# A new hand-off list for the first three blocks of a fused retention and snake-MLP kernel

## The chip, the cores and the metric

One NeuronCore of a Trainium2 chip runs the whole kernel. The metric is the device time of one execution in microseconds. The engines are named as in the profile: PE (TensorE, matmuls), PEld (its weight loads), DVE (VectorE), ACT (ScalarE), POOL (GpSimd) and SP (SyncE, which here only issues DMAs). Each engine works through its own instructions in order.

## The reference

`q`, `k` and `v` have 8 batches, 8 heads, 576 positions and 64 features, in float32. The first part is retention (attention without softmax, with a decay); its output is the input of the second part, a dense MLP with a snake activation:

```python
scores = scale * np.matmul(q, k.transpose(0, 1, 3, 2))
gamma = 1.0 - 2.0 ** (-5.0 - np.arange(H, dtype=np.float32))
Dmat = np.where(rel >= 0, gamma[:, None, None] ** rel[None, :, :], 0.0)
x = np.matmul(scores * Dmat, v)          # then transposed to 4608 tokens x 512
h = x @ w_in                             # 512 -> 2048
s = np.sin(alpha * h)
g = h + s * s / (alpha + 1e-09)
out = g @ w_out                          # 2048 -> 512
```

## The kernel before

The 4608 tokens are worked off in nine blocks of 512. Blocks 0 to 7 are the first 512 positions of each batch; block 8 gathers the last 64 positions of all batches. All matmuls are in float16 with float32 sums in PSUM.

**Attention of one block** (class `Attention`). A half `p` of a block is 256 positions. `load` brings q, k or v of a half in (SP's queue, 512 KB) and `cast` multiplies it by powers of the decay and by the scale and writes float16 (for v it is a copy alone); the argument `ys` casts one half of the heads. In blocks 0 and 1 `turn` transposes q and k on TensorE and `take` copies the result out of PSUM; from block 2 on `crossed` has the DMA transpose them. `scores` multiplies k and q, `masked` applies the causal mask on VectorE, `outer` makes the sums of k times v per chunk of 128 positions, `take_sum`, `evict` and `evict_bank` bring these to SBUF, `more` (GpSimd) or `next_sum` (VectorE) adds the decayed sum of the chunk before, and `to_state` writes the state in float16. `values` and `add_states` add up the output in PSUM, and `keep` copies it to SBUF as x of the block.

**MLP of one block.** A unit is 128 of the 2048 hidden columns. `project(n, u, bank)` is four matmuls of 512 columns (or two halves of 256), `sine` runs on ScalarE, `square` on an engine that the list names, `product` on VectorE, and it frees the unit's PSUM bank. `gemm2(n, u, bank)` is one quarter of the sum of one output tile of 128 tokens (tile `u // 4`, hidden units `4 * (u % 4)` to `4 * (u % 4) + 3`); `finish` copies the tile out and stores it.

**PSUM** has six tags: `op`, `h0`, `h1`, `h2` are one bank each, `m0` and `m1` two banks each. A tile with a tag waits until what stood there was read.

**The order.** For blocks 0 to 2 everything above is written out as one list of calls, inside `tc.manual_schedule()`: each engine gets its instructions in the list's order, and waits between engines are put in from the data. From block 3 on a loop makes the order; it is the same before and after. Buffers in SBUF are taken in the order in which the list asks for them, by the table `BUFFERS`: the digit is the number of the buffer. `load_w_in(g)` and `load_w_out(g)` bring a quarter of the weights each through GpSimd's queue, with a cast to float16 on the way. `wait_for_w_in(g)` and `wait_for_w_out(g)` are tiny DMAs on SP that read the loaded weights, so that SP's later loads stay behind them. `keep_busy` are matmuls on zeros at the start, when TensorE has nothing to do.

Of the kernel before, what the change touches and what calls it, by code (L numbers as in the profile page):

```python
# [19 lines left out]
    "raw": "012345012345012345102405314023140240124012401240",  # L20
    "k16": "0123012302131313",
    "q16": "0120120121202020",
    "v16": "0123012310230123",
    "kT": "0123012310232323",
    "qT": "0123013210232323",
    "kvs": "00000000",
    "s16": "01010101",
    "xT": "01202020",
    "s32": "010101010101010101010",
    "ret": "01230123012313020213021302130213",  # L30
    "s": "012312013021302130210213021302130231032032103102320132013201320132013201320132013201320132013201320132013201320132013201320132013201320132013201",
    "ss": "012302130123012032103213021302103210321031203120312031203120312031203120312031203120312031203120312031203120312031203120312031203120312031203120",
# [4 lines left out]
def kernel(  # L37
# [23 lines left out]
    P = 128  # L61
# [221 lines left out]
    class Attention:  # L283
# [83 lines left out]
        def more(self, c):  # L367

            s32 = place("s32", [P, 4, D], F32)
            nc.gpsimd.tensor_tensor(s32, self.kvs[:, c - 1], g1.unsqueeze(2).to_broadcast([P, 4, D]), MULT)  # L370
            nc.gpsimd.tensor_tensor(self.kvs[:, c], s32, self.kvs[:, c], ADD)  # L371
# [180 lines left out]
    ops = {}  # L552
    PART = {None: slice(0, 512), 0: slice(0, 256), 1: slice(256, 512)}
# [46 lines left out]
    def gemm2(n, u, tag, cols=slice(0, 512)):  # L600
        c, part = divmod(u, 4)
        if (n, c, cols.start) not in ops:
            ops[n, c, cols.start] = psum.tile([P, 512], F32, tag=tag, bufs=1, name="ops")
        for fk in range(4 * part, 4 * part + 4):
            matmul(  # L605
                ops[n, c, cols.start][:, cols], gT[n][:, fk, c * P : (c + 1) * P], w_out16[:, fk, cols],
                start=(fk == 0), stop=(fk == FC - 1), skip_group_check=True,
            )
# [127 lines left out]
    def wait_for_w_in(g):  # L736

        nc.sync.dma_start(gate, w_in16[g][:, 0, 0:64])
# [42 lines left out]
    with tc.manual_schedule():  # L781
# [27 lines left out]
        at[0].outer((0,), "h1", "h2")  # L809
        keep_busy(8, "op", 256)  # L810
        cast(0, "k", 1, G_, (1,))
        take(0, "k", 0, A_)
        take(0, "q", 0, A_)
        at[0].scores(0, 0, "m0")
        at[0].scores(0, 1, "m1")
# [5 lines left out]
        turn(0, "k", 1, "op")  # L821
        take(0, "k", 1, A_, (0,))
        take(0, "k", 1, A_, (1,))
        turn(0, "q", 1, "h0")
        take(0, "q", 1, A_)
        keep_busy(3, "op")
        at[0].scores(1, 0, "m1")
        keep_busy(1, "h1")
# [8 lines left out]
        take(1, "q", 1, A_)  # L837
        at[0].masked(0, 1)
        at[0].next_sum(1)
        at[0].to_state(1, G_)  # L840
        load_w_out(2)
        at[0].outer((1,), "h2", "h0")
        at[0].take_sum(3, A_)
        at[0].masked(0, 0)
        at[0].values(0, False, "m1")
        at[0].values(0, True)
        at[0].masked(1, 0)
        at[0].masked(1, 1)
        at[0].next_sum(2)
        at[0].to_state(2, V)  # L850
        at[0].add_states(0)
        at[0].keep(0, A_, V)
        at[0].values(1, False, "h1", "h0")
        at[0].values(1, True)
        at[0].add_states(1)
        load(1, "q", 0)
        cast(1, "q", 0, G_)
        load_w_in(3)
        turn(1, "q", 0, "op")
        at[0].keep(1, V, A_)  # L860
        take(1, "q", 0, V)
        project(0, 2, "h2", 0)
        project(0, 3, "m0", 0)
        project(0, 2, "h2", 1)
        sine(0, 2)
        project(0, 3, "m0", 1)
        sine(0, 3)
        square(0, 3, V)
        product(0, 3)
        project(0, 1, "h0", 0)  # L870
        project(0, 1, "h0", 1)
        sine(0, 1)
        square(0, 1, V)
        square(0, 2, A_)
        product(0, 2)
        product(0, 1)
        project(0, 6, "h1")
        sine(0, 6)
        project(0, 7, "m1")
        sine(0, 7)  # L880
        project(0, 0, "op")
        square(0, 7, A_)
        sine(0, 0)
        square(0, 6, V)
        product(0, 7)
        product(0, 6)
# [568 lines left out]
```

## Time and profile before

| what | value |
|---|---|
| median of three runs | 295.57 us (295.13 to 298.53) |
| profiled execution | 295.48 us |
| its span, first to last instruction | 293.8 us |
| granted TensorE clock | 0.998 |
| busy: PE, DVE, ACT, POOL | 282.6, 227.5, 206.4, 135.2 us |
| first projection of block 0 | 21.0 us |
| DMA | 50.08 MB, mean 170 GB/s |

Busy is the sum of an engine's instructions, waits left out. The rows of groups have the form: line, engine, operation, what is written and read with shapes, count, then busy us and mean ns, then idle us before them and what ended most of it. In a timeline a row begins with its start and its length.

### The profile page before, as it was taken

How to read it: one execution, taken by the hardware profiler on the slowest of the kernel's cores; microseconds unless marked ns; L12 is line 12 of the kernel's file. 1: busy time of each engine (PE TensorE's matmuls, PEld its weight loads, DVE VectorE, ACT ScalarE, POOL GpSimd, SP SyncE). 2: the span in 40 equal slices, each digit the busy share in tenths (PEclk: the TensorE clock that was granted, in tenths of full speed). 3: DMA queues.
4: the chain of work that ended last, by engine and by line, in shares of the span. 5: the costliest groups of instructions: out<-in, count | busy, mean ns of one | idle time of the engine just before them, and what ended most of it. 6: DMA issues, size and time to landing. Idle time of an engine off the chain costs nothing. (4 is left out here: it accounts for less than half of the span.)

```text
span 293.8 us, 8462 instructions
## 1 busy us (share of the span) xinstructions
PE 282.6 (96%) x3480; PEld 182.6 (62%) x3480; DVE 227.5 (77%) x336; ACT 206.4 (70%) x340; POOL 135.2 (46%) x152
## 2 busy tenths in 40 slices
PE   6789999999998999999999999999999999999994
PEld 4566555555544654455767777676666676777783
DVE  2597968788349979698987697769777987987784
ACT  2679945997594896787867986797678657865500
POOL 6694776475689576640397039802960000000000
PEclk9999999999999999999999999999999999999999
DMA  7999999999798899968868976897764102111213
GB/s 218 347 235 211 249 292 309 235 261 291 184 219 199 155 173 190 284 120 174 158 160 237 138 190 155 252 126 178 183 176 60 40 9 83 36 38 36 71 38 107
DMA packets 122918, 50.08 MB, mean 170 GB/s; under 512 B 79872, under 2 KB 120832, under 8 KB 122880
## 3 DMA queue, kind: packets, MB, share of 16 engines
q1 hardware_dynamic: 118928, 44.78, 63.8%
q0 software_dynamic: 2688, 4.19, 7.9%
q10 hardware_dynamic: 1264, 0.58, 0.8%
q8 instruction: 27, 0.44, 0.6%
q14 instruction: 11, 0.09, 0.1%
HBM read 36.75 MB, written 9.44 MB: 157 GB/s over the span
## 5 line engine op out<-in xcount | busy, mean ns | idle before, releaser
L592 DVE SCALAR_TENSOR_TENSOR gT<-ss,inva,hps 128x512 f16<-128x512 f16 x144 | 105.4, 743 | 29.7 <-ACT ss L585 26.0
L576 ACT ACTIVATE s<-hps,alpha_t 128x512 f16<-128x512 f32 x144 | 96.6, 681 | 44.7 <-PE hps L568 42.7
L568 PE MATMUL hps<-xT,w_in 128*128 128x512 f16 (+1 forms) x532 | 121.1, 372 | 1.2 <-DMA w_in<-in_moe_w_in_dram 0.6
L568 PEld LDWEIGHTS <-w_in 128*128 128x128 f16 x596 | 66.6, 114 | 51.0 <-issue 1.4
L585 ACT ACTIVATE ss<-s 128x512 f16<-128x512 f16 x106 | 66.6, 631 | 2.8
L605 PE MATMUL ops<-w_out,gT 128*128 128x512 f16 x192 | 46.8, 380 | 0.0
L671 PEld LDWEIGHTS <-gT 128*128 128x128 f16 x384 | 37.5, 98 | 8.3
L207 POOL TENSOR_TENSOR k<-raw,cn 128x1024 f16<-128x1024 f32 (+1 forms) x17 | 28.6, 1682 | 9.7 <-DMA raw<-in_k_dram 9.7
L671 PEld LDWEIGHTS <-S 128*128 128x128 f16 x288 | 27.7, 98 | 5.3
L605 PEld LDWEIGHTS <-gT 128*128 128x128 f16 x192 | 18.0, 98 | 20.5
L363 POOL TENSOR_TENSOR s<-kvs,cn 128x256 f16<-128x256 f32 x17 | 10.8, 639 | 38.7 <-DVE S L652 24.7
L207 POOL TENSOR_TENSOR q<-raw,cn 128x1024 f16<-128x1024 f32 x13 | 24.8, 1912 | 5.8 <-DMA raw<-in_q_dram 4.1
L671 PE MATMUL hps<-T,gT 128*128 128x256 f16 x192 | 22.9, 273 | 0.0
L671 PE MATMUL hps<-w_out,gT 128*128 128x256 f16 x192 | 22.9, 273 | 0.0
L671 PE MATMUL hps<-w_out,S 128*128 128x256 f16 x192 | 22.8, 273 | 0.0
L401 DVE TENSOR_TENSOR ret<-sc,mask 128x1024 f16<-128x1024 f32 x16 | 19.1, 1218 | 2.1 <-PE sc L389 2.0
L120 ACT CAST xT<-o 128x1024 f16<-128x1024 f32 (+1 forms) x15 | 16.5, 1128 | 2.7 <-PE o L451 2.7
L587 DVE TENSOR_TENSOR ss<-s 128x512 f16<-128x512 f16 x29 | 14.7, 509 | 3.2 <-ACT s L576 3.1
L371 POOL TENSOR_TENSOR kvs<-s,kvs 128x256 f32<-128x256 f32 x21 | 15.3, 730 | 2.8 <-DVE kvs L122 1.2
L717 DVE TENSOR_TENSOR osb<-hps,low 128x512 f32<-128x512 f32 x13 | 9.0, 692 | 9.3 <-PE hps L671 9.3
L370 POOL TENSOR_TENSOR s<-kvs,cn 128x256 f32<-128x256 f32 x21 | 13.3, 634 | 6.2 <-ACT kvs L120 6.0
L652 DVE TENSOR_TENSOR S<-gT,S 128x1024 f16<-128x1024 f16 x24 | 15.5, 683 | 0.0
(83 smaller groups left out, 272.2 us busy)
## 6 DMA issues: line engine op xcount, KB each, us to landing
raw<-in_q_dram SPq DMA_DIRECT2D x16, 512.0 KB, 4.9
out_dram<-osb SPq DMA_DIRECT2D x32, 256.0 KB, 2.5
raw<-in_k_dram SPq DMA_DIRECT2D x8, 512.0 KB, 6.4
raw<-in_v_dram SPq DMA_DIRECT2D x8, 512.0 KB, 5.9
raw<-in_v_dram SPq DMA_DIRECT2D x32, 128.0 KB, 3.2
raw<-in_k_dram SPq DMA_DIRECT2D x32, 128.0 KB, 3.1
w_in<-in_moe_w_in_dram POOLq DMA_DIRECT2D x4, 512.0 KB, 11.7
w_out<-in_moe_w_out_dram POOLq DMA_DIRECT2D x4, 512.0 KB, 13.0
```

Source lines behind the costliest of these rows:

```text
L120: eng.copy(d_, s_)
L207: eng.tensor_tensor(dst[:, a0:a1].rearrange("p a r t d -> p t (a r) d"), t_.rearrange("p (t a) x -> p t a x", t=2)[:, :, a0:a1].rearrange( ...
L371: nc.gpsimd.tensor_tensor(self.kvs[:, c], s32, self.kvs[:, c], ADD)
L401: nc.vector.tensor_tensor(ret.rearrange("p t (z x) -> p (t z) x", z=2)[:, :, 0:n], sc.rearrange("p t (z x) -> p (t z) x", z=2)[:, :, 0:n], ...
L568: matmul(hps_of[n, fc][0][:, cols], w_in16[fc // 4][:, a, fc % 4 :: 4], xs[n][:, a, cols], start=(a == 0 and part != 1), stop=(a == KT - 1 ...
L576: nc.scalar.activation(s_t, hps, mybir.ActivationFunctionType.Sin, bias=0.0, scale=alpha_t[:, fc : fc + 1],)
L585: nc.scalar.activation(ss_t, s_t, mybir.ActivationFunctionType.Square)
L587: eng.tensor_tensor(ss_t, s_t, s_t, MULT)
L592: nc.vector.scalar_tensor_tensor(gT[n][:, fc, :], ss_t, inva[:, fc : fc + 1], hps, MULT, ADD)
L605: matmul(ops[n, c, cols.start][:, cols], gT[n][:, fk, c * P : (c + 1) * P], w_out16[:, fk, cols], start=(fk == 0), stop=(fk == FC - 1), sk ...
L652: return eng.tensor_tensor(out_, x, y, op)
L671: matmul(acc[:, 256 * j : 256 * j + 256], lhs[:, x, 128 * j : 128 * j + 128], rhs[:, x], start=(tag is not None and j == js[0] and p == 0 ...
```

## The change

The list of blocks 0 to 2 is replaced by another one, found by a search over a model of the engines and queues. The same calls are in it, with these differences. The loads of block 0 come in another order. GpSimd issues the first three groups of w_in after half a cast of q instead of after k's casts. VectorE casts k of block 0 and, later on, parts of k and q of blocks 2 to 4; casts are more often halved. VectorE has 16 squares instead of 11, ScalarE 23 instead of 28, GpSimd 9 as before. VectorE makes three of the chunk sums (`more` gets an engine) and seven states instead of one. Units, `gemm2` quarters and attention steps follow one another in another order and on other banks; `gemm2` may now add up its four quarters in any order. Buffers get other numbers. `make_mask_halved` moves from the start to block 1. The loop from block 3 on, and the tail, are not touched.

```diff
 BUFFERS = {
-    "raw": "012345012345012345102405314023140240124012401240",
+    "raw": "423104350312251304250124323152014240124012401240",
...
-        def more(self, c):
+        def more(self, c, eng=nc.gpsimd):
             s32 = place("s32", [P, 4, D], F32)
-            nc.gpsimd.tensor_tensor(s32, self.kvs[:, c - 1], g1.unsqueeze(2).to_broadcast([P, 4, D]), MULT)
-            nc.gpsimd.tensor_tensor(self.kvs[:, c], s32, self.kvs[:, c], ADD)
+            eng.tensor_tensor(s32, self.kvs[:, c - 1], g1.unsqueeze(2).to_broadcast([P, 4, D]), MULT)
+            eng.tensor_tensor(self.kvs[:, c], s32, self.kvs[:, c], ADD)
...
+        done = parts_of.setdefault((n, c), [])
+        done.append(part)
         for fk in range(4 * part, 4 * part + 4):
             matmul(
                 ops[n, c, cols.start][:, cols], gT[n][:, fk, c * P : (c + 1) * P], w_out16[:, fk, cols],
-                start=(fk == 0), stop=(fk == FC - 1), skip_group_check=True,
+                start=(len(done) == 1 and fk == 4 * part), stop=(len(done) == 4 and fk == 4 * part + 3),
+                skip_group_check=True,
             )
...
-        keep_busy(7, "op", 128)
-        keep_busy(6, "h0", 256)
-        keep_busy(11, "op", 128)
-        make_mask_halved()
-        load(0, "k", 0)
-        load(0, "q", 0)
-        load(0, "v", 0)
-        cast(0, "k", 0, V, (0,))
-        cast(0, "k", 0, G_, (1,))
-        turn(0, "k", 0, "op")
-        cast(0, "q", 0, V, (1,))
-        cast(0, "q", 0, V, (0,))
-        turn(0, "q", 0, "h0")
-        load(0, "k", 1)
-        cast(0, "k", 1, G_, (0,))
-        invert_alpha()
-        cast(0, "v", 0, A_)
...
-        cast(0, "k", 1, G_, (1,))
...
-        load(0, "q", 1)
-        load_w_in(0)
-        load(0, "v", 1)
-        at[0].take_sum(0, A_)
-        cast(0, "q", 1, V)
...
-        cast(0, "v", 1, A_)
-        load(1, "q", 1)
-        cast(1, "q", 1, G_)
-        at[0].scores(1, 1, "m0")
-        turn(1, "q", 1, "h1")
...
+        load(0, "k", 0)
+        keep_busy(4, "h1", 256)
+        cast(0, "k", 0, V, (0,))
+        cast(0, "k", 0, V, (1,))
+        turn(0, "k", 0, "h0")
+        keep_busy(13, "op", 128)
+        keep_busy(5, "op", 128)
+        load(0, "q", 0)
+        cast(0, "q", 0, V, (1,))
+        load(0, "q", 1)
+        cast(0, "q", 0, G_, (0,))
+        load(0, "k", 1)
+        load_w_in(0)
+        turn(0, "q", 0, "h2")
+        load(0, "v", 0)
+        load(0, "v", 1)
+        take(0, "k", 0, V, (0,))
+        take(0, "k", 0, V, (1,))
+        cast(0, "q", 1, V, (1,))
+        load_w_in(1)
+        load_w_in(2)
+        cast(0, "q", 1, V, (0,))
...
+        cast(0, "k", 1, V, (0,))
+        cast(0, "k", 1, V, (1,))
...
+        cast(0, "v", 0, G_, (0,))
+        cast(0, "v", 0, G_, (1,))
+        cast(0, "v", 1, G_, (0,))
...
+        load(1, "q", 1)
+        cast(0, "v", 1, A_, (1,))
+        at[0].take_sum(1, A_)
+        at[0].take_sum(0, V)
+        at[0].more(1)
...
+        at[0].to_state(0, A_)
+        at[0].take_sum(2, A_)
+        at[0].more(2)
...
+        at[0].to_state(2, V)
+        at[0].values(1, False, "m0")
+        at[0].add_states(0)
+        wait_for_w_in(0)
+        at[0].values(1, True)
+        at[0].add_states(1)
+        load(1, "k", 0)
+        at[0].keep(0, V, A_)
+        at[0].keep(1, V, A_)
+        project(0, 3, "h1", 0)
+        project(0, 3, "h1", 1)
+        load(1, "q", 0)
+        cast(1, "q", 1, V)
+        invert_alpha()
...
+        at[1].take_sum(2, A_)
+        at[1].masked(1, 1)
+        at[1].more(2, V)
+        load(2, "q", 1)
+        make_mask_halved()
+        at[1].to_state(2, V)
+        gemm2(0, 14, "h2")
...
+        finish(0, 3, V)
+        at[1].to_state(3, V)
+        cast(2, "q", 0, V, (1,))
+        cast(2, "k", 0, V)
+        square(1, 14, V)
+        product(1, 14)
+        cast(2, "k", 1, G_)
+        cast(2, "q", 0, G_, (0,))
...
```

More of the change, by code (lines that the diff above doesn't have):

```diff
@@ new lines @@
+        cast(3, "k", 0, G_, (0,))
+        at[2].to_state(2, G_)
+        cast(3, "v", 0, G_, (1,))
+        crossed(3, 1, "k")
+        at[2].to_state(3, G_)
+        cast(3, "v", 1, G_, (1,))
+        cast(3, "v", 1, G_, (0,))
+        crossed(3, 1, "q")
+        load(4, "q", 1)
+        finish(0, 2)
+        product(1, 1)
+        square(1, 5, A_)
+        product(1, 5)
+        sine(1, 15)
+        square(1, 15, A_)
+        sine(1, 12)
+        sine(1, 2)
+        square(1, 12, A_)
+        at[2].masked(0, 1)
@@ new lines @@
+        gemm2(1, 3, "h2")
+        gemm2(1, 2, "h2")
+        at[3].more(1, V)
+        project(2, 6, "m1")
+        sine(2, 7)
+        load(4, "k", 1)
+        crossed(3, 0, "k")
+        load(4, "v", 1)
+        finish(1, 1)
+        wait_for_w_in(3)
+        crossed(3, 0, "q")
+        finish(1, 3)
+        load(4, "v", 0)
+        square(2, 7, V)
+        sine(2, 2)
+        sine(2, 1)
+        at[3].more(2)
+        sine(2, 4)
+        square(2, 1, A_)
+        at[3].to_state(1, V)
+        product(2, 7)
@@ L1182 @@
[L1182 to L1186 removed]
+        gemm2(1, 8, "op")
+        gemm2(1, 11, "op")
+        gemm2(1, 1, "h2")
+        project(2, 10, "h1")
+        at[3].scores(0, 0, "m1")
+        at[3].values(1, False, "m0")
+        gemm2(1, 10, "op")
+        project(2, 13, "h2")
+        at[3].scores(0, 1, "m1")
+        at[3].values(1, True)
+        at[3].add_states(1)
+        project(2, 3, "h1")
+        load(4, "q", 0)
```

728 lines of the change are left out of this document (336 added, 392 removed).

## The prediction

> **What bounds the kernel now.** I read the page first, then the busy time by stretches, then the timeline of TensorE, then the groups of VectorE. The page says that TensorE sets the time; its VectorE row shows where that is in danger (40 slices of 7.3 us each, tenths busy).
>
> ```profile
> span 293.8 us, 8462 instructions
> PE 282.6 (96%) x3480; PEld 182.6 (62%) x3480; DVE 227.5 (77%) x336; ACT 206.4 (70%) x340; POOL 135.2 (46%) x152
> DVE  2597968788349979698987697769777987987784
> ```
>
> The timeline of TensorE tells when real work begins and at what pace it then runs: start, length, line, operation, count, and in brackets the idle time before it and what ended it.
>
> ```profile
> 19.81 0.62 PE L240 MATMUL tr<-ident,q 128*128 128x128 f16 x8
> 21.01 8.86 PE L568 MATMUL hps<-xT,w_in 128*128 128x256 f16 x56 [0.57 <-DMA w_in<-in_moe_w_in_dram]
> 100.75 5.37 PE L568 MATMUL hps<-xT,w_in 128*128 128x512 f16 x24
> ```
>
> A projection unit is four 512-column matmuls. The last row, 24 of them in 5.37 us with the last one's drain of some 0.2 us inside, gives 0.216 us each, 0.87 us a unit. At 21.01 the first projection starts; the first 56 (32 half-width, 24 full) would take 32 x 0.108 + 24 x 0.216 = 8.6 us and the drain, and took 8.86: full pace. So from 21 us on TensorE hardly waits, and the first 21 us, where one attention block goes by in a chain of small steps, are the largest stretch in which it does little. The unchanged loop from block 3 on begins inside the row at 100.75, after five units, at 105.1 us. What the change can touch is therefore 0 to 105 us: at most a few us of the start, and stalls added to a stretch that now has few.
>
> The busy time by stretches (length; then busy us of PE, weight loads, DVE, ACT, POOL with counts; granted clock, DMA share, GB/s):
>
> ```profile
> 21.00:48.00 27.00, 26.87 (x349) 15.94 (x350) 20.54 (x30) 17.59 (x32) 17.39 (x19) 1.00 1.12 260
> 48.00:75.00 27.00, 26.60 (x388) 14.72 (x387) 22.80 (x34) 22.64 (x36) 15.26 (x17) 1.00 1.03 265
> 75.00:105.00 30.00, 29.13 (x334) 15.06 (x333) 19.80 (x25) 22.79 (x45) 24.06 (x24) 1.00 0.84 186
> 105.00:109.30 4.30, 4.30 (x22) 2.13 (x20) 3.94 (x8) 4.27 (x10) 3.70 (x5) 1.00 0.98 166
> ...
> 90.00:100.00 10.00, 9.34 (x173) 4.89 (x175) 10.00 (x12) 6.35 (x13) 7.74 (x9) 1.00 0.87 180
> ```
>
> VectorE works 20.54 + 22.80 + 19.80 + 3.94 = 67.1 us between the first projection and 109.3 us, where its last product of block 2 ends: 76% of 88.3 us, 21.2 us idle. In the one stretch where it is full (90 to 100: 10.00 of 10) TensorE loses most, 0.66 us by this busy time.
>
> **The change, the start.** SP issues the loads now as k0, q0, q1, k1, v0, v1 (before k0, q0, v0, k1, q1, v1). VectorE casts both halves of k0 and of k1, one half of q0 and both of q1, where GpSimd did k1 and half of k0; GpSimd's first task is half of q0, and then it issues w_in, three groups, before it casts v. The building of the halved mask leaves GpSimd's start for block 1; it stands there behind the state sums and nothing of block 0 to 3 reads it, so it costs nothing as long as GpSimd has idle time (27.00 - 15.26 us in the middle stretch); without that, its memset and four selects (1.02 us, first row below) delay the casts behind them by a little more than that.
>
> ```profile
> 3.41 1.02 POOL L776 TENSOR_SCALAR_AFFINE_SELECT mask_halved<-mask_halved 64x128 f16<-64x128 f16 x4
> 4.77 0.69 DVE L207 TENSOR_TENSOR k<-raw,cn 128x512 f16<-128x512 f32 x1 [3.54 <-DMA raw<-in_k_dram]
> 6.42 1.29 DVE L207 TENSOR_TENSOR q<-raw,cn 128x512 f16<-128x512 f32 x2 [0.95 <-DMA raw<-in_q_dram]
> 9.45 2.04 POOL L207 TENSOR_TENSOR k<-raw,cn 128x512 f16<-128x512 f32 x2 [3.08 <-DMA raw<-in_k_dram]
> 10.96 1.61 DVE L207 TENSOR_TENSOR q<-raw,cn 128x1024 f16<-128x1024 f32 x1 [2.87 <-DMA raw<-in_q_dram]
> ...
> 6.43 1.45 SPq L158 DMA_DIRECT2D raw<-in_v_dram  x1
> 10.98 1.32 SPq L158 DMA_DIRECT2D raw<-in_k_dram  x1
> 11.43 2.43 POOL L110 DMA_DIRECT2D w_in<-in_moe_w_in_dram  x3
> 21.39 1.90 POOL L207 TENSOR_TENSOR k<-raw,cn 128x1024 f16<-128x1024 f32 x1 [0.60 <-DMA raw<-in_k_dram]
> ```
>
> Each cast that waited for a load gives its landing: first load 4.77, second 6.42, fourth 9.45, fifth 10.96, so one load every (10.96 - 4.77)/4 = 1.55 us. The sixth, v1, issued at 6.43, would land at 12.5 undisturbed, 6.1 us after its issue. The two last rows of the second group show what w_in does to a load beside it: block 1's k, issued at 10.98, should land at 17.1, but w_in was issued 0.45 us behind it, and it landed at 21.39, 4.3 us late. Now w_in is issued when GpSimd's half cast ends, 6.42 + 1.02 = 7.45 at best (8.0 if VectorE's cast beside it slows it by half). That is 1.0 to 1.6 us behind v1's issue, so between two thirds and a quarter of v1's 1.55 us still falls under w_in: 2.8 to 1.1 us late, v1 at 13.6 to 15.3; I take 14.3. Ends: 12.5 (no overlap) and 16.8 (the whole 4.3).
>
> w_in itself then lands some 8 us after its issue instead of 9.6, near 16, and is no longer the last thing awaited. In the kernel before it was, but only by 0.57 us; early weights alone buy no more than that. SP's queue holds a wait for w_in's first group behind block 1's first q load, and its next two loads stand behind that wait to about 16 us: their users on GpSimd stand behind a square of the first units and a state sum, past 22 us, so it costs nothing; should w_in land at 21 as before, the loads would come some 6 us later than that wait's end, near 27, and GpSimd, with block 0's later squares queued behind, would be up to 4 us late.
>
> What is late next is v1. Behind it stands block 0's state chain, and its terms are these:
>
> ```profile
> L120 ACT CAST v<-raw 128x512 f16<-128x512 f32 x1 | 0.6, 607 | 0.0
> L120 ACT COPY kvs<-kv 128x256 f32<-128x256 f32 x4 | 1.5, 380 | 3.5 <-PE kv L325 3.5
> L370 POOL TENSOR_TENSOR s<-kvs,cn 128x256 f32<-128x256 f32 x12 | 7.8, 650 | 6.2 <-ACT kvs L120 6.0
> L371 POOL TENSOR_TENSOR kvs<-s,kvs 128x256 f32<-128x256 f32 x12 | 8.8, 732 | 2.1 <-DVE kvs L122 1.2
> 19.09 0.42 DVE L363 TENSOR_TENSOR s<-kvs,cn 128x256 f16<-128x256 f32 x1
> 19.25 0.63 PE L451 MATMUL o<-qT,s 64*64 64x128 f16 x16
> ```
>
> ScalarE's half cast of v1 0.61 (ScalarE's first `take_sum` is queued behind this cast, and GpSimd's `more(1)` behind both), the sum's copy 0.38, `more(1)` 0.65 + 0.73, `more(2)` the same, `to_state(2)` 0.42, `add_states` 0.63, `keep` 0.74 (row below): 5.54, and seven handovers, which I put at 0.05 each: 5.9 us. x is whole at 14.3 + 5.9 = 20.2; the first half unit (0.43 us) can go ahead, so projections effectively begin at 19.8. Before it was 21.01 with two transposes of block 1 already done, which now come later and take about 0.5 us each (0.62 with the drain): 20.0 in the same terms. The start gains 0.2 us; with the ends of v1, from 2.0 gained to 2.3 lost.
>
> **The change, blocks 0 to 2.** TensorE's work is the same (32 `gemm2` quarters, 48 units, the same attention), and the reordered accumulation of `gemm2` adds no instruction. Squares, evictions, states and casts move from ScalarE and GpSimd to VectorE. Its groups in this stretch:
>
> ```profile
> L592 DVE SCALAR_TENSOR_TENSOR gT<-ss,inva,hps 128x512 f16<-128x512 f16 x49 | 35.0, 743 | 12.7 <-ACT ss L585 9.9 <-POOL ss L587 2.5
> L401 DVE TENSOR_TENSOR ret<-sc,mask 128x1024 f16<-128x1024 f32 x12 | 14.4, 1218 | 1.7 <-PE sc L389 1.7
> L587 DVE TENSOR_TENSOR ss<-s 128x512 f16<-128x512 f16 x12 | 5.8, 492 | 3.1 <-ACT s L576 3.1
> L642 DVE TENSOR_TENSOR T<-w_out 128x1024 f16<-128x1024 f16 x2 | 3.2, 1597 | 0.0
> L122 DVE CAST xT<-o 128x512 f16<-128x512 f32 x3 | 2.2, 737 | 0.1
> L207 DVE TENSOR_TENSOR k<-raw,cn 128x1024 f16<-128x1024 f32 x1 | 2.0, 1997 | 0.0
> L122 DVE COPY osb<-ops 128x512 f32<-128x512 f32 x2 | 1.4, 683 | 2.3 <-PE ops L605 2.3
> L354 DVE SCALAR_TENSOR_TENSOR kvs<-kvs,cn,kv 128x64 f32<-128x64 f32 x4 | 0.8, 268 | 0.0
> L122 DVE COPY kT<-tr 128x1024 f16<-128x1024 f16 x1 | 0.7, 685 | 0.0
> ```
>
> From the new list, from the first projection to the loop: 48 products 35.7; 12 masks 14.6; 16 squares 7.9; 3 whole casts between 1.22 and 2.00, 4.8; 5 half casts at 0.69, 3.5; 2 `take` 1.4; 5 `keep` halves 3.7; 4 `finish` 2.7 and 2 bank evictions of the same size 1.4; 6 `to_state` at 0.42, 2.5; 3 `more`, never seen on VectorE, at two of the nearest row (0.42), 2.5 (end: GpSimd's 1.38 each, 4.1); `next_sum` 1.1; two weight sums 3.2; a sum copy and alpha 0.8. Sum 85.8 us, 18.7 more than before, 97% of the 88.3 us.
>
> VectorE is in order: its list can begin when `keep` ends, at 20.2, and so ends at 106.0 plus its waits. Before it waited 21.2 us, most of it for squares (12.7 in the first row). Waits shrink when work is queued, but the list does not start full: the first product needs a sine and square behind the first unit. Ends: 0 and 21.2; I take 8, nearer the full stretch (no wait in 10 us) than the mean. End at 114.0 against 109.3, 4.7 us late. One unit (0.87 us) of that is covered by the spare PSUM bank that TensorE has; the rest is late on TensorE, because every projection needs a bank that a product frees. So +3.8, the 0.2 of the start being in it. ScalarE and GpSimd become lighter, which costs and pays nothing here. The other buffer numbers and banks bring loads no nearer than SP allows: block 2's first load now waits for the casts of block 1's v, with all loads of block 2 queued behind it on SP; its cover is `gemm2` of block 0, of which nine quarters (9 x 0.87 = 7.8 us) stand behind that point, and a v later than that costs its excess in full.
>
> The profiled execution took 295.48 us, 1.7 around its span of 293.8, and the median is 295.57: 295.5 + 3.8 = **299.3 us**.
>
> **Rivals.**
>
> *The start pays and VectorE packs (293.5 us, chance 0.22).* v1 lands at 12.5, x is whole at 18.4, and VectorE's waits fall to about 5: 18.4 + 85.8 + 5 = 109.2, on time, so TensorE keeps its 2.0 us. For it: squares now come from three engines and most old waits were for squares. Against it: the 4.3 us that w_in cost the load beside it.
>
> *VectorE and GpSimd block each other (305.3 us, chance 0.28).* The mechanism is a wait inside instructions that read two SBUF operands:
>
> ```profile
> 88.69 2.39 DVE L642 TENSOR_TENSOR T<-w_out 128x1024 f16<-128x1024 f16 x1
> 92.80 0.80 DVE L642 TENSOR_TENSOR T<-w_out 128x1024 f16<-128x1024 f16 x1
> 88.52 2.02 POOL L207 TENSOR_TENSOR q<-raw,cn 128x1024 f16<-128x1024 f32 x1 [1.49 <-DMA qT<-q]
> 45.62 1.22 DVE L207 TENSOR_TENSOR q<-raw,cn 128x1024 f16<-128x1024 f32 x1
> ```
>
> The same weight sum takes 0.80 alone and 2.39 under a GpSimd cast; a whole cast 1.22 and 2.00. Casts, squares, `more`, `to_state` and weight sums read two such operands: 15 in this stretch before, 8 + 16 + 6 + 6 + 2 = 38 now. Excess before: 1.6 + 0.8 + 12 x 0.07 = 3.2 us, 0.21 each; 38 of them are 8 us, of which my row means hold about 4. If GpSimd is the busier neighbour at the new casts and the rest is 6 us: 20.2 + 85.8 + 8 + 6 = 120.0, 10.7 late, less 0.87: +9.8. It decides once VectorE's waits and excess pass 10 us. Against it: GpSimd gives up casts of about 4.5 whole tiles of k and q, at 1.9 us some 8.6 us. [...]
>
> *Early w_in does nothing by itself* is part of the forecast: only 0.57 us waited for it.
>
> **How the numbers follow.** Forecast, 299.3 with 296.5 to 303.5: 0.50, of which 0.18 lies above 301.5, 2% over the median, about what a measurement of this kernel can tell from no change. First rival 0.22, reaching 291 if the remaining small stalls go too; 0.07 of it below 289.7. Second 0.28, reaching 307.5 when v1 is at 16.8 as well; 0.26 above 301.5. Faster 0.07, same 0.32 + 0.15 + 0.02 = 0.49, slower 0.18 + 0.26 = 0.44. Range 291.0 to 307.5.
>
> **What would show it.** Right: VectorE over 90% from 21 to 105 us, TensorE's idle rows there ended by products, v1's cast waiting for its load until 13.6 to 15.3, the first projection at 19 to 20. Wrong: v1 cast before 13 and the loop reached before 105 (first rival), squares and half casts on VectorE well over 0.5 and 0.7 us (second), or TensorE waiting for loads or transposes by DMA in block 2 or 3, which I hold to be on time.

## Result and profile after

The new list takes 305.53 us (median of four runs, 302.77 to 306.38) against 295.47: ratio 1.0301, 95% interval 1.0204 to 1.0398. The forecast was 299.3 with 291.0 to 307.5. The number lies inside the range, near the second rival's 305.3, but the runs below show that most of the way there is another one. The kernel after was run four times more (e8); its eight times spread from 302.77 to 306.38, which is as much as most of the edits below are worth, so a single profiled run shows where time goes better than how much.

The page of the kernel after: span and instructions, busy time of the engines, then VectorE and the granted clock in 40 slices, of 7.6 us here.

```profile
span 304.5 us, 8450 instructions
PE 286.3 (94%) x3468; PEld 181.7 (60%) x3468; DVE 242.6 (80%) x359; ACT 201.7 (66%) x337; POOL 127.2 (42%) x151
...
DVE  3857998796678799789897589759975997996884
...
PEclk9977999999999999999999999999999999999998
```

The span is 10.7 us longer. VectorE is not full in blocks 0 to 2 (from 23 to 114 us, slices 4 to 15, four of the twelve digits are a nine), and the clock row has two sevens that the kernel before did not have. The busy time by stretches (length; busy us of TensorE, weight loads, VectorE, ScalarE, GpSimd with counts; clock, DMA share, GB/s) puts numbers to both:

```profile
21.00:116.00 95.00, 88.71 (x1075) 46.38 (x1075) 77.06 (x112) 60.45 (x104) 56.35 (x68) 0.97 0.96 220
...
16.20:18.00 1.80, 0.00 (x0) 0.00 (x0) 1.06 (x1) 1.48 (x6) 1.64 (x3) 1.00 1.18 212
...
19.40:26.30 6.90, 6.22 (x23) 3.28 (x23) 3.30 (x6) 2.79 (x4) 1.64 (x2) 0.51 1.16 277
```

VectorE is busy 81% of the 95 us that the forecast filled to 97%. TensorE does nothing from 16.2 to 18.0 us, and from 19.4 to 26.3, just when the projections begin, its clock is at half. The timeline of TensorE after (start, length, line, operation, count, idle time before and its end) shows the rest:

```profile
15.77 0.41 PE L430 MATMUL o<-ret,v 64*64 64x128 f16 x14 [0.16 <-issue]
18.01 0.47 PE L430 MATMUL o<-ret,v 64*64 64x128 f16 x18 [1.83 <-issue]
...
20.93 11.12 PE L570 MATMUL hps<-xT,w_in 128*128 128x256 f16 x45 [0.18 <-ACT xT L120]
...
37.94 0.42 PE L389 MATMUL sc<-qT,kT 64*64 64x128 f16 x16 [1.31 <-DVE gT L594]
70.83 0.42 PE L389 MATMUL sc<-qT,kT 64*64 64x128 f16 x16 [1.67 <-DMA qT<-q]
86.11 0.44 PE L325 MATMUL kv<-v,k 64*64 64x64 f16 x32 [1.11 <-POOL v L122]
```

Four places carry most of the loss, none of them a full VectorE. At 18.01 TensorE resumes in the middle of one step (14 of its 32 matmuls were done) after 1.83 us in which it waited for nothing that the profile names. At 20.93 the row with 45 projection matmuls takes 11.12 us. At 37.94 a product of VectorE is late. At 70.83 and 86.11 operands of blocks 2 and 3 are late.

How late TensorE is I took from its own work: each matmul counted at its full-speed length, fillers left out, and the times compared at which the sum so far is the same as in the kernel before. The table has the profiled runs of the new list and its variants, e12 left out; the times in the heading are in the run named at the left.

| late by (us) at | 28 | 40 | 56 | 68 | 116 |
|---|---|---|---|---|---|
| after | 3.1 | 5.4 | 6.7 | 6.3 | 10.7 |
| after, again (e8) | 4.6 | 7.0 | 8.3 | 9.9 | 10.4 |
| fillers (e1) | 1.3 | 3.0 | 4.5 | 4.6 | 5.7 |
| late w_in (e2) | 2.7 | 5.5 | 6.8 | 6.9 | 7.7 |
| square on ScalarE (e3) | 3.8 | 5.5 | 6.9 | 6.8 | 10.8 |
| raw buffers (e4) | 3.9 | 6.1 | 7.5 | 7.1 | 7.9 |
| VectorE loaded (e6) | 2.8 | 6.6 | 8.3 | 9.7 | 11.1 |
| GpSimd exchange (e7) | 3.3 | 4.4 | 5.5 | 5.7 | 6.8 |
| e1 + e4 + e7 (e9) | 1.5 | 3.5 | 5.0 | 4.6 | 5.4 |
| e9 + e2 (e11) | 1.3 | 3.3 | 4.8 | 4.5 | 5.2 |

From 116 us on none of them changes by more than 0.1.

### The profile page after: what moved, and what is told of

It is laid out like the page before. It is cut to its first block, busy times and chain, and to the rows that moved or that the text cites. A ratio compares the mean times of both kernels' runs of the same rounds, so it can differ in the third digit from the quotient of the medians.

```text
span 304.5 us, 8450 instructions
## 1 busy us (share of the span) xinstructions
PE 286.3 (94%) x3468; PEld 181.7 (60%) x3468; DVE 242.6 (80%) x359; ACT 201.7 (66%) x337; POOL 127.2 (42%) x151
## 5 line engine op out<-in xcount | busy, mean ns | idle before, releaser
L570 PE MATMUL hps<-xT,w_in 128*128 128x512 f16 (+1 forms) x524 | 125.8, 382 | 2.2 <-ACT xT L120 0.8
L587 ACT ACTIVATE ss<-s 128x512 f16<-128x512 f16 x101 | 63.3, 631 | 4.8 <-DVE gT L594 2.4
L676 PEld LDWEIGHTS <-S 128*128 128x128 f16 x288 | 27.7, 98 | 5.3
L207 POOL TENSOR_TENSOR k<-raw,cn 128x512 f16<-128x512 f32 (+1 forms) x17 | 24.8, 1469 | 12.6 <-DMA raw<-in_k_dram 9.5
L363 POOL TENSOR_TENSOR s<-kvs,cn 128x256 f16<-128x256 f32 x14 | 8.7, 622 | 40.2 <-DVE S L657 38.0
L207 POOL TENSOR_TENSOR q<-raw,cn 128x512 f16<-128x512 f32 (+1 forms) x14 | 21.4, 1547 | 6.6 <-DMA raw<-in_q_dram 6.6
L589 DVE TENSOR_TENSOR ss<-s 128x512 f16<-128x512 f16 x34 | 19.1, 562 | 3.6 <-ACT s L578 3.1
L589 POOL TENSOR_TENSOR ss<-s 128x512 f16<-128x512 f16 x9 | 9.4, 1041 | 22.6 <-ACT s L578 20.0
L370 POOL TENSOR_TENSOR s<-kvs,cn 128x256 f32<-128x256 f32 x20 | 12.9, 643 | 8.0 <-DVE kvs L371 4.3
```

Of the source, the lines that this page charges most:

```text
L207: eng.tensor_tensor(dst[:, a0:a1].rearrange("p a r t d -> p t (a r) d"), t_.rearrange("p (t a) x -> p t a x", t=2)[:, :, a0:a1].rearrange( ...
L370: eng.tensor_tensor(s32, self.kvs[:, c - 1], g1.unsqueeze(2).to_broadcast([P, 4, D]), MULT)
L570: matmul(hps_of[n, fc][0][:, cols], w_in16[fc // 4][:, a, fc % 4 :: 4], xs[n][:, a, cols], start=(a == 0 and part != 1), stop=(a == KT - 1 ...
L587: nc.scalar.activation(ss_t, s_t, mybir.ActivationFunctionType.Square)
L589: eng.tensor_tensor(ss_t, s_t, s_t, MULT)
L676: matmul(acc[:, 256 * j : 256 * j + 256], lhs[:, x, 128 * j : 128 * j + 128], rhs[:, x], start=(tag is not None and j == js[0] and p == 0 ...
```

## Experiments: the start

**e1, TensorE kept busy at 16 to 18 us.**

```diff
+        keep_busy_m(8, "m0")          # 8 zero matmuls of 512 columns
         at[0].values(0, True)         # both moved behind masked(1, 0)
```

> The kernel after with one addition: eight zero matmuls of 512 columns into bank m0, and values(0, True) moved behind masked(1, 0), so that TensorE has work where it stood idle from 16.18 to 18.01 us. Theory A (clock): that idle gap is what halved the granted clock from 19.50 to 26.33 us; matmuls that took 216 ns took 427 ns there, and TensorE lost about 3 us by 28 us. With the gap filled the clock stays full, and the time falls by 2.5 to 3.2 us, to about 302.7. Theory B (the forecast's own: VectorE's list sets how late TensorE is): the time TensorE loses at the half clock would be waited for anyway, and the time changes by less than 0.5 us. If the gap is a wait for TensorE's own instructions, the added matmuls stand behind that wait too, the gap stays, the half clock stays, and the time rises by up to 1 us.

304.06 us (301.17 to 305.68). The timeline of TensorE in e1:

```profile
16.39 1.89 PE L740 MATMUL idle<-zero 128*128 128x512 f16 x8 [0.57 <-DVE ret L401]
...
21.70 8.57 PE L570 MATMUL hps<-xT,w_in 128*128 128x256 f16 x45 [0.38 <-ACT xT L120]
```

In this profiled run the gap is gone, no half clock follows, and the same 45 matmuls take 8.57 us instead of 11.12: 2.6 us, the first theory's size. The fillers cost 0.77 us themselves (the row begins at 21.70 instead of 20.93), and by 28 us TensorE is 1.8 us less late than in the kernel after. The median moved only 1.5, since two of the four runs took 305.3 and 305.7: their mean granted clock was 0.992 and 0.988, against 1.00 in the other two. The fillers seem to keep the clock up in some executions and not in others; the two slower ones were not profiled.

**e2, w_in issued 5 us later**, which is the position of the early load tested in the new list.

```diff
-        load_w_in(0) ... load_w_in(1), load_w_in(2)   # behind GpSimd's half of q0
+        load_w_in(0), load_w_in(1), load_w_in(2)      # behind cast(0, "v", 1, G_, (0,))
```

> The kernel after with w_in issued where GpSimd has cast its half of v1, about 13.4 us, instead of 8.25 us. Theory A (early w_in is what starves TensorE of instructions): TensorE's second block of instructions, fetched at 15.67 us in the kernel after and at 14.07 us in the kernel before, comes by 14.3 us again, the idle gap from 16.18 to 18.01 us goes, and the clock stays full; w_in lands at about 21 us and takes back 1 to 1.6 us of the 3, so the time falls by about 1.5 us, to 304. Theory B (w_in early is a plain gain, as the forecast had it): the time rises by 0.5 to 1.6 us with w_in's landing.

303.63 us (303.17 to 305.57). w_in is issued at 13.19, TensorE's stall shrinks, and no projection waits for the weights:

```profile
13.19 2.42 POOL L110 DMA_DIRECT2D w_in<-in_moe_w_in_dram  x3
15.90 0.47 PE L430 MATMUL o<-ret,v 64*64 64x128 f16 x18 [1.00 <-issue]
...
19.71 0.37 PE L570 MATMUL hps<-xT,w_in 128*128 128x256 f16 x1 [0.21 <-DVE xT L122]
```

The median fell as far as the first theory said, but not on its road: the stall went from 1.83 to 1.00 us, the clock still halved, from 18.6 to 25.5 us, and by 28 us TensorE is only 0.4 us less late. The rest of this run's gain lies after 68 us, where executions differ anyway (see e4). The page of the kernel after has 27 records of 16 KB on an instruction queue (q8) for TensorE's 6936 matmuls and weight loads, so one for about 256 of them: I read them as refills of its instructions. The queue view shows the one in question. These are the queues' rows (packets, MB, share of 16 engines) of the kernel before from 14.0 to 15.1 us, of the kernel after from 12.9 to 15.6 and from 15.6 to 16.7, and of e2 from 13.6 to 14.6.

```profile
q1 hardware_dynamic: 717, 0.36, 109.2%
q8 instruction: 1, 0.02, 5.4%
```

```profile
q0 software_dynamic: 422, 0.42, 91.1%
q1 hardware_dynamic: 319, 0.16, 29.1%
...
q0 software_dynamic: 145, 0.15, 79.3%
q1 hardware_dynamic: 146, 0.07, 33.6%
q8 instruction: 1, 0.02, 5.4%
```

```profile
q8 instruction: 1, 0.02, 5.9%
q1 hardware_dynamic: 26, 0.01, 3.4%
```

TensorE had issued its 256th matmul or weight load at 13.5 us in the kernel before and at 13.2 after; the refill began 0.5 us later there and 2.5 us later here, while w_in's packets (the q0 row) filled the engines. In e2, with w_in late, it was 1.1 us. What starts a refill is not shown (in e10 it begins when 245 are issued), so these delays are rough. In the kernel after, its repetition and e2 the refill begins at 15.67, 16.71 and 13.62 and TensorE resumes at 18.01, 19.09 and 15.90: 2.3 to 2.4 us behind it each time. And it stops at the same place, behind its 449th instruction (in the kernel after 445 of them are matmuls and weight loads), in all seven profiled runs of the new list without fillers, for 0.9 to 2.0 us. That TensorE waits for its own instructions is read from these two regularities.

**e5, early w_in alone, in the kernel before.**

```diff
+        load_w_in(0), load_w_in(1), load_w_in(2)
         cast(0, "k", 1, G_, (0,))
...
-        load_w_in(0) ... load_w_in(1), load_w_in(2)   # further down
```

> The kernel before with one part of the change alone: the three loads of w_in are issued ahead of GpSimd's casts of block 0's k1, at about 6.4 to 8.5 us instead of 11.43. The forecast priced early weights at a gain of 0.57 us at most, less what they take from the loads beside them. Theory A (the early w_in holds up the other transfers of the start, TensorE's instructions among them): k1 and v1 land up to 4.3 us later and TensorE's second block of instructions, which came 0.5 us after its index was passed, comes 2 us or more after it; TensorE stands longer near 14 to 18 us, the granted clock may halve, and the time rises by 1 to 4 us, to 296.5 to 299.5. Theory B (early weights are a plain gain): 294.8 to 295.5.

305.91 us, ratio 1.0336 (1.0287 to 1.0385): one part of the change, moved by itself, costs as much as all of it, and far more than I expected. The timeline of e5:

```profile
6.68 2.43 POOL L110 DMA_DIRECT2D w_in<-in_moe_w_in_dram  x3
...
20.47 1.04 ACT L120 CAST v<-raw 128x1024 f16<-128x1024 f32 x1 [3.78 <-DMA raw<-in_v_dram]
23.66 1.90 POOL L207 TENSOR_TENSOR q<-raw,cn 128x1024 f16<-128x1024 f32 x1 [11.79 <-DMA raw<-in_q_dram]
25.61 1.03 PE L240 MATMUL tr<-ident,q 128*128 128x128 f16 x8 [8.74 <-POOL q L207]
```

v1, issued at 6.79, lands at 20.45, and block 1's q, issued at 8.42, at 23.6: 14 and 15 us, where the loads issued ahead of w_in landed after 4.2 to 6.1. TensorE's list holds a transpose of that q ahead of block 0's last steps, so TensorE stands 8.74 us. In the kernel after, the list is built around the early load: block 0's six loads are issued before it (v1 lands at 12.7), and block 1's first tile, issued at 9.54, lands at 22.17 with nothing of TensorE waiting. So there the price is only what late w_in gives back: 0.4 us at 28 us in e2, 0.75 us on the median in e11.

**e10, the clock by itself: the kernel before without its last twelve fillers.**

```diff
-        keep_busy(8, "op", 256)
-        keep_busy(3, "op")
-        keep_busy(1, "h1")
```

> The kernel before without its last twelve filler matmuls (eight of 256 columns near 10 us, three and one of 512 columns near 14 to 16 us); no result is computed from them. This is the dispute over the clock by itself, in the other kernel: Theory A (idle time of TensorE at the start halves its rate for some us after): matmuls of 512 columns take about 0.43 us instead of 0.216 in a stretch of 3.4 or 6.8 us near 20 us, and the time rises by 1.5 to 3.5 us, to 297 to 299. Theory B (the half rate in the kernel after comes from something else, its early w_in or its order): the rate stays full and the time stays within 0.5 us of 295.6.

295.44 us against 295.19: ratio 1.0004 (0.9984 to 1.0023). My expectation was wrong. The timeline of TensorE:

```profile
12.08 1.03 PE L240 MATMUL tr<-ident,k 128*128 128x128 f16 x8
...
20.72 0.62 PE L240 MATMUL tr<-ident,q 128*128 128x128 f16 x8
...
21.66 8.72 PE L568 MATMUL hps<-xT,w_in 128*128 128x256 f16 x55 [0.21 <-DVE xT L122]
```

The half rate is there: eight transposes take 1.03 us until 18 us and 0.62 from 20.7; without the fillers the rate rises at 20.4 us, where it rose at 12.8 in the kernel before. But it costs nothing, because TensorE, with work in 4.5 of the 4.7 us from 16 to 20.7, is back at the full rate when the projections begin, and the small steps before stretch where TensorE would else have waited or run fillers. So idle time at the start is not the loss. The loss is a half rate that reaches into the dense stretch.

**e8, the kernel after once more.**

> The kernel after, unchanged, beside the others, since its time spreads from 302.8 to 306.4. Theory A (clock and loads): its granted clock halves near 19 us in every run, TensorE stands from about 16.2 to 18 us for its own instructions, and the stalls at 69 and 85 us come in some executions and not in others, with the time 303 to 306. Theory B (VectorE): these places are the same in every execution, since VectorE's list is, and the spread is elsewhere.

304.64 us (303.13 to 306.19). The projections run at half rate again, but not because the clock halved near 19 us. The stretch from 21 to 27.7 us, and two rows of TensorE:

```profile
21.00:27.70 6.70, 6.03 (x31) 3.13 (x23) 3.46 (x6) 2.32 (x4) 1.16 (x2) 1.00 1.05 277
```

```profile
13.29 1.04 PE L240 MATMUL tr<-ident,k 128*128 128x128 f16 x8
...
22.80 10.85 PE L570 MATMUL hps<-xT,w_in 128*128 128x256 f16 x45 [0.17 <-ACT xT L120]
```

The view gives the clock as 1.00, but the 45 matmuls take 10.85 us, and 512-column matmuls start every 0.43 us until 27.7. The rate is read better from the matmuls: the clock's record in this trace has its first entry at 27.65 us, and before it the view shows 1.00. Eight transposes already take 1.04 us at 13.29, as at the half rate of e10. So this execution had no full rate before 27.7 us, where the profiled kernel after had it from 9.3 to 19.5; here the gap cannot have taken it away. Too little work of TensorE before the projections would fit both, but was not tested by itself. The profiled runs agree on the fillers: in e1, e9, e11 and e12, which have them, the projections start at full rate, in the seven of the new list without them at half. This run is 4.6 us late at 28 us instead of 3.1 and makes it good later: the waits at 69 and 85 us are absent. Where the loss falls differs from run to run.

## Experiments: blocks 0 to 2

**e3, one square on ScalarE.**

```diff
-        square(0, 7, V)
+        square(0, 7, A_)
```

> The kernel after with one square, of unit 7 of block 0, on ScalarE instead of VectorE. In the kernel after it took 2.49 us under two casts of GpSimd (0.49 us is the mean of such squares before), and TensorE then waited 1.31 us for the product behind it and fell from 3.2 to 5.2 us late. Theory A (VectorE and GpSimd shut each other out in instructions with two SBUF operands): that step goes, and 1.5 to 2 us of time with it, to about 304. Theory B (VectorE's list as a whole sets the lateness, so that 2 us saved at one place are waited for at the next): under 0.5 us.

303.52 us (302.49 to 306.24). VectorE's square and GpSimd's casts in the kernel after, and then what took its place in e3:

```profile
34.61 2.49 DVE L589 TENSOR_TENSOR ss<-s 128x512 f16<-128x512 f16 x1
34.77 2.04 POOL L207 TENSOR_TENSOR k<-raw,cn 128x512 f16<-128x512 f32 x2
```

```profile
36.14 0.57 ACT L120 COPY qT<-tr 128x512 f16<-128x512 f16 x1
36.60 0.63 ACT L587 ACTIVATE ss<-s 128x512 f16<-128x512 f16 x1
...
37.27 2.06 DVE L594 SCALAR_TENSOR_TENSOR gT<-ss,inva,hps 128x512 f16<-128x512 f16 x3 [1.76 <-ACT ss L587]
```

TensorE's loss from 34 to 40 us fell only from 2.2 to 1.5 us, and at the end this run was as late as the kernel after. On ScalarE the square waits behind another square and a copy, and VectorE waits for it. A miss for the first theory as a remedy; as a mechanism the square needed another test.

**e7, the same square freed by an exchange on GpSimd.**

```diff
+        load_w_out(2)
         cast(1, "k", 1, G_, (0,))
         cast(1, "k", 1, G_, (1,))
-        load_w_out(2)
```

> The kernel after with one exchange on GpSimd: the issue of w_out's third group, 0.6 us, goes ahead of the two half casts of block 1's k1, so that these begin some 0.6 us after VectorE's square of unit 7 rather than with it. [...] Theory B: whatever the square takes, TensorE waits there for something else, and it is as late at 40 us as before, within 0.5 us.

302.26 us (301.66 to 303.91), 2.4 below the kernel after on the same chip and the best single edit.

```profile
34.91 1.04 DVE L589 TENSOR_TENSOR ss<-s 128x512 f16<-128x512 f16 x1
35.04 0.59 POOL L113 DMA_DIRECT2D w_out<-in_moe_w_out_dram  x1
...
36.85 0.42 PE L389 MATMUL sc<-qT,kT 64*64 64x128 f16 x16
```

The square takes 1.04 instead of 2.49, the matmuls of the scores no longer wait, and TensorE loses 0.9 us instead of 2.2 from 34 to 40 (at 40 it is 1.0 less late, where the second theory allowed 0.5): the second rival's mechanism, shown at one place, at 1.3 us. The whole trace of the kernel after has it too, in VectorE's instructions with two operands in SBUF: the 23 squares with no instruction of GpSimd beside them take 0.36 to 0.43 us, the nine that lie for over 70% of their time under GpSimd's 0.42 to 2.49; half casts 0.68 to 0.69 alone and up to 1.10; a weight sum 0.69 alone and 1.92. The products, with one operand in PSUM, take 0.73 to 0.75 either way (72 alone, 59 under GpSimd's instructions). GpSimd's own half casts of q take 1.04 alone, and one beside a cast of VectorE 1.45. The square is held up for more than one instruction of GpSimd: in the kernel after it ends 0.3 us behind the second of two casts in a row (37.10 against 36.81). In e7 it ends 0.3 us behind the issue of w_out (35.95 against 35.63), before which GpSimd did a square of its own.

**e4, block 2's loads freed from block 1's v.**

```diff
-    "raw": "423104350312251304250124323152014240124012401240",
+    "raw": "423104350312450312451042343054102421042104210421",
```

> The kernel after with the raw buffers renumbered from the second load of block 2 on, so that this load no longer waits for the cast of block 1's v (in the kernel after SP stood 9.3 us there, until 46.99 us, and every load of blocks 2 and 3 came behind it). Theory A (the loads are late): SP goes on at about 27 to 35 us, the waits of TensorE for the transposes of block 2 (1.67 us at 69 us) and for the casts of v of block 3 (1.11 us at 85 us) go, and the time falls by 2.5 to 3.5 us, to about 302.5. Theory B (the forecast's: loads are on time, VectorE sets the lateness): under 0.5 us of change.

303.30 us (301.96 to 304.72). SP's waits in the kernel after hold the row that the edit removes; the timeline of GpSimd gives block 2's k cast in the kernel after and in e4:

```profile
SPq L158 <- ACT v L120: 9.3, 1, 9.3
```

```profile
57.84 1.91 POOL L207 TENSOR_TENSOR k<-raw,cn 128x1024 f16<-128x1024 f32 x1 [4.73 <-DMA raw<-in_k_dram]
```

```profile
52.41 1.90 POOL L207 TENSOR_TENSOR k<-raw,cn 128x1024 f16<-128x1024 f32 x1
```

The cast comes 5.4 us earlier without a wait, and TensorE loses 0.8 us from 68 to 116 instead of 4.4. But e1, e2, e7 and e8 lose no more than 1.1 there with the old buffers. So the late loads take away the slack, and whether the transposes then come late changes between executions; the table shows 4 us in two of the six runs with the old buffers and the list otherwise nearly unchanged (after, e3). That the edit is worth the 2.2 us between the medians is not shown.

**e6, VectorE loaded with 8.7 us more.**

```diff
         product(0, 3)                 # and 31 others
+        nc.vector.memset(spare, 0.0)
```

> The kernel after with 32 memsets of a spare 128x512 f16 tile on VectorE, one behind each product of blocks 0 and 1, at 0.27 us each (the memset of 128x512 f16 at the start took 272 ns): 8.7 us more for VectorE between 21 and 105 us, and no other work or wait. Theory A (the forecast's main term: VectorE's list sets TensorE's lateness, its waits being 8 us): nearly all of it passes on, plus 5 to 8.7 us, 310 to 314. Theory B (VectorE has 18 us idle of 95 there, and TensorE was late through single places, not through VectorE's total): plus 0 to 2.5 us, 305 to 308.

307.30 us (305.87 to 307.40), 2.7 above the kernel after on the same chip and 1.8 above its first median: a fifth to a third of the 8.7 reached the end. Where there is no slack more of it does: from 28 to 68 us, with 18 of the 32 memsets (4.9 us), this run loses 6.9 us by the table, the two profiled runs of the kernel after 3.2 and 5.3.

**e9, three edits together** (e1, e4 and e7).

> The kernel after with three edits together: the eight filler matmuls (e1), the renumbered raw buffers (e4) and the exchange on GpSimd's queue (e7). Theory A (three separate places: half clock about 3 us, the blocked square 1.3 to 2.4 us, late loads 0 to 3 us): the gains add, and the time falls by 4.5 to 6.5 us from the 304.6 of the kernel after, to 298 to 300. Theory B (one resource, VectorE, sets the lateness, and a place made shorter is waited for at the next): no more than the best single edit brought, 302 or more.

301.59 us (300.37 to 303.72): 3 us of the 4.5 to 6.5 that the first theory added up. One reason is in its trace. With the full clock everything comes earlier, and the square of unit 7 is caught again:

```profile
32.95 2.37 DVE L589 TENSOR_TENSOR ss<-s 128x512 f16<-128x512 f16 x1
...
36.16 0.42 PE L389 MATMUL sc<-qT,kT 64*64 64x128 f16 x16 [1.05 <-DVE gT L594]
```

What is gained at one place shifts the phase of the next: the square takes 2.49 us in the kernel after, 1.04 in e7, 2.37 here.

**e11, late w_in besides** (e2).

> The three edits of e9 and late w_in (e2) together. Theory A (early w_in holds up block 1's first loads, which landed at 22.2 and 25.3 us, and TensorE's instructions at 15.7 us): both come earlier, the start loses another 0.5 to 1 us less, and the time is 0.5 to 1.5 us below e9's, near 298. Theory B (w_in is what the first projections wait for when it is issued at 13.4 us): 0.5 to 1.5 us above e9's. Neither is expected to reach the 295.6 of the kernel before, since the losses from 48 to 64 us, about 2 to 2.5 us, are untouched.

300.84 us (300.51 to 301.94, and one of the six runs 306.00), 0.75 below e9: the first theory's sign and, at its lower end, its size, with ranges that overlap. No version found beats the kernel before. Of the 5 us that remain here, 1.3 are lost by 28 us, 2 more by 40 and 1.5 by 56; causes of the last were not tried singly.

**e12, all sixteen VectorE squares of blocks 0 to 2 on ScalarE besides.**

```diff
-        square(0, 3, V)               # and fifteen others
+        square(0, 3, A_)
```

> The kernel of e11 with all sixteen squares of blocks 0 to 2 that VectorE does given to ScalarE. In the kernel after they take 10.8 us on VectorE, 4.0 us more than sixteen at 0.42, because some stand under GpSimd's instructions (2.37 us under GpSimd in e9 where TensorE then waited 1.05 us); on ScalarE they take 0.63 each, 10 us for an engine that is idle for 35 of 95 us there. Theory A (VectorE's squares under GpSimd are what the stretch from 30 to 64 us still loses): 1.5 to 3 us below e11's 300.8, 298 to 299.3. Theory B (a square gains nothing on another engine whose queue it joins, as the single one of e3 did, 0.5 us locally): within 0.7 us of e11, or slower by up to 2 us where ScalarE's sines come later. The 295.2 of the kernel before is reached by neither.

317.38 us (315.38 to 318.82): both theories missed. Stretches from the first projection to the end of the 48th product, the last of block 2, in the kernel after, in e6, in e11 and in e12:

```profile
19.38:119.37 99.99, 93.02 (x1093) 48.49 (x1093) 81.16 (x119) 64.55 (x114) 57.40 (x69) 0.97 0.97 217
```

```profile
20.39:119.77 99.38, 92.34 (x1097) 47.93 (x1094) 88.90 (x151) 64.65 (x114) 57.00 (x69) 0.98 0.92 216
```

```profile
20.17:113.92 93.75, 89.97 (x1093) 47.34 (x1093) 80.97 (x119) 64.46 (x114) 59.27 (x69) 1.00 0.94 232
```

```profile
20.03:125.73 105.70, 92.15 (x1090) 47.70 (x1090) 72.67 (x103) 73.48 (x130) 57.82 (x70) 0.99 0.89 217
```

The sixteen squares took 9.1 us of VectorE in e11. Without them VectorE works 8.3 us less on these blocks (80.97 to 72.67), they end 11.8 us later, and the time rose by 16.5; with 8.7 us more on VectorE it had risen by 2 to 3. VectorE's total alone does not set the time. In e12 what does is when each product's square is done, and the groups of VectorE from 21 to 116 us in e11 and in e12 show it (busy us, mean ns; idle time before them and what ended it):

```profile
L594 DVE SCALAR_TENSOR_TENSOR gT<-ss,inva,hps 128x512 f16<-128x512 f16 x49 | 35.4, 743 | 3.0 <-ACT ss L587 1.5 <-POOL ss L589 1.0
```

```profile
L594 DVE SCALAR_TENSOR_TENSOR gT<-ss,inva,hps 128x512 f16<-128x512 f16 x41 | 29.6, 744 | 22.3 <-ACT ss L587 20.8 <-POOL ss L589 1.3
```

In e12 the products wait 20.8 us for squares that stand behind sines and copies in ScalarE's queue, although ScalarE is busy 73.48 of 105.70 us there, 70%, hardly more than the 69% of e11.

## Why the prediction was right and wrong

**v1 late, taken at 14.3: wrong.** GpSimd's half cast of q0 took 1.45 us, not 1.02, so w_in was issued at 8.25, and v1, a load issued at 6.81, was through at 12.74, near the end of 12.5 that the forecast kept. The forecast's step to two thirds or a quarter of v1's 1.55 us does not follow from its own 1.0 to 1.6 us either: what these leave of 1.55 is a third or nothing, which gives 12.5 to 14.0. The first projection began at 19.38, inside 19 to 20. I had looked only at whether the load ahead of w_in is late, and not at TensorE's instructions, whose packets stand on the same 16 engines (the q8 row, 5.4% of them from 15.6 to 16.7 us).

**The start, a gain of 0.2 with 2.0 gained and 2.3 lost as ends: a term was missing.** The clock stood at 1.00 in every stretch quoted from before, and I never asked what would make it fall. When TensorE stopped at 16.2 us it was 1.6 us ahead, behind the stop it was 0.4 late, and by 28 us 3.1. So the stop cost 2.0 us and the half rate 2.7, of which the row of 45 matmuls is 2.6, by e1. In the profiled run of the kernel after the whole loss is 3.1 us by 28 us, 3.2 from there to 68 and 4.4 from 68 to 116 (4.6, 5.3 and 0.5 in e8), where the forecast had a gain of 0.2, a loss of 4.0 by VectorE, and nothing for late loads.

**x whole 5.9 us behind v1, `keep` 0.74 in parallel: wrong.** ScalarE's half waits for VectorE's half of the same two-bank tile:

```profile
20.14 0.73 ACT L120 CAST xT<-o 128x512 f16<-128x512 f32 x1 [0.78 <-DVE xT L122]
```

So x was whole at 20.87, 8.1 us behind v1. The handovers were as short as the forecast's 0.05 us: this row begins 0.03 us behind VectorE's half, and the projections 0.06 us behind it (20.93). The other 1.4 us of the difference were not taken apart; TensorE's stop lies in this stretch.

**VectorE's list of 85.8 us with 8 us of waits: the step that failed.** From the first projection to the end of the 48th product VectorE worked 81.2 us and stood idle 18.8 (the first row of e12's section), hardly less than the 21.2 before. Its waits for squares did shrink, from 12.4 to 3.0 us. What stands there now are waits for TensorE's results (7.8, before 5.1), for loads (3.2, before none) and for sines (3.1 as before), while TensorE's own waits for products of VectorE add up to 2.1 us: VectorE waited for the others more than they for it. The forecast passed VectorE's lateness on almost in full; e6 passed on a fifth to a third, and e12 went the other way. The range holds the result by luck: its upper part rests on the second rival, whose VectorE ends at 120.0 with 93.8 us of work and 6 of waits, where the trace has 119.4 with 81.2 and 18.8.

**One VectorE square against one GpSimd cast (second rival): right as a mechanism, wrong in how it adds up.** It came to 305.3 by 8 us of excess in VectorE's total. The group of VectorE's squares from 0 to 116 us shows half of that, for sixteen of the 38 instructions it counted:

```profile
L589 DVE TENSOR_TENSOR ss<-s 128x512 f16<-128x512 f16 x16 | 10.8, 673 | 3.5 <-ACT s L578 3.1
```

Against 0.42 us each that is 4.1 us too much for sixteen, and what reached TensorE was 1.3 us at one place (e7).

**Loads on time: wrong, in some executions.** In the profiled run SP stood 9.3 us at the buffer of block 1's v, longer than the 7.8 us of cover. The waits at 70.83 and 86.11 are the sign that the forecast had named for this. **The halved mask, and SP's wait for w_in at no cost: right**; no row of TensorE waits behind them. **Early weights buy nothing: right, and too mild**: alone they cost 10.3 us in the kernel before (e5).

## What to carry to other kernels

Before moving a large transfer earlier, list every transfer that will share the engines with it, an engine's own instructions among them, and who waits in order for each; moved by itself this one cost 10 us, with the list built around it less than 1 (e11). An engine's total says little once three in-order engines hand each unit on: ask for each instruction which one it stands behind, since 9 us of squares taken off the busiest helper cost 16.5. And look whether TensorE is at its full rate when the dense work begins (the same 45 matmuls took 8.57 us at it and 11.12 at half), not how much idle time there is before (e10).

## What the hardware showed

- Around TensorE's gap of 1.83 us in the kernel after and 1.75 us in e4 its clock fell to half, for 6.8 us from 19.5, behind the gap, and for 10.2 us from 16.9, inside it: twice and three times the 3.4 us of e6's shortest stretch (at full from 14.5 to 17.9). What makes it fall, and in which executions, was not shown by itself: in the kernel after TensorE worked in the 1.5 us between the gap's end and the fall (1.24 of the 1.40 us from 18.0 to 19.4).
- The clock in a view can mislead: e8's record begins with a rise at 27.65 us, and the view has 1.00 before it, with matmuls at 0.43 us.
- TensorE's instructions came in what I read as refills of about 256 (27 records on q8 for 6936). The one under w_in's traffic began 2.5 us behind the 256th instruction in the kernel after, 0.5 us in the kernel before and 0.4 in e11, with w_in late; TensorE then stopped for up to 2.0 us.
- Loads of 512 KB issued just before or beside w_in took 12 to 15 us instead of 4 to 6. From 12 to 20 us the engines moved 216 GB/s in the kernel after and 279 in the kernel before, at the same busy share (1.20 and 1.19); w_in was in flight in both, in the kernel before from 11.4 us, and what makes the difference was not shown by itself:

```profile
DMA packets 2212, 1.73 MB, mean 216 GB/s; under 512 B 41, under 2 KB 2211, under 8 KB 2211
```

```profile
DMA packets 3750, 2.24 MB, mean 279 GB/s; under 512 B 71, under 2 KB 3749, under 8 KB 3749
```
